# Top-k attention and SwiGLU on one core: the fourth FFN block's gate and value computed in halves of 128 tokens

## The chip, the core and the metric

One core of one Trainium2 chip runs the whole program. The metric is device microseconds for one execution of the kernel, from a median of a few runs. The engines that matter are PE (TensorE, the matrix engine, whose weight loads are listed apart as PEld), DVE (VectorE), ACT (ScalarE), POOL (GpSimd) and SP (SyncE, which here issues nearly all DMAs). Each engine executes its own list of instructions in the order in which the program wrote them, and waits where an instruction needs the result of another engine.

## The reference

Everything is fp32. For 8 batches of 8 heads, 576 positions and head size 64, each row of scores keeps its 32 largest entries and is softmaxed over these. The result, laid out as 4608 tokens of 512 features, goes through a gated feed-forward network of width 1536.

```python
def _attn_ref(q, k, v):                       # (8, 8, 576, 64) each
    scores = scale * np.matmul(q, k.transpose(0, 1, 3, 2))
    kth = np.partition(scores, -top_k, axis=-1)[..., -top_k:-top_k + 1]   # top_k = 32
    scores = np.where(scores >= kth, scores, -1000000000.0)
    scores = scores - np.max(scores, axis=-1, keepdims=True)
    attn = np.exp(scores)
    attn = attn / (np.sum(attn, axis=-1, keepdims=True) + 1e-09)
    return np.matmul(attn, v)

def _moe_ref(x, w_gate, w_val, w_out):        # x: (4608, 512), d_ff = 1536
    g = x @ w_gate
    silu = g * (1.0 / (1.0 + np.exp(-g)))
    val = x @ w_val
    return silu * val @ w_out
```

## The kernel before

**Attention in units.** The attention is cut into 160 units (`units`, line 281): 8 batches, 5 query tiles each (four of 128 rows, and a last one of 64), and 4 pairs of heads. A full unit handles two heads of 128 query rows; a unit of the last query tile packs two heads of 64 rows and is called a half unit here (one 576-wide row set in place of two). The loop at line 870 walks over the units. In turn `n` DVE selects the top 32 of unit `n` (`select`, lines 347 and 351: four rounds of MAX8 with three rounds of MATCH_REPLACE8 between them), ACT turns the scores of unit `n-1` into exponentials (`weigh`, lines 374 and 379), DVE and POOL or ACT normalize them (`normalize`, lines 392 to 399), and PE transposes the weights of unit `n-2` (`turn`, line 412). Every second turn, the even ones, PE also computes the scores of the next two units (`scores`, lines 325 and 308) and the products with V of the units `n-4` and `n-3` (`values`, line 448). ACT copies these last into the token buffer `xT` (line 465).

**FFN in blocks and pieces.** The 4608 tokens form 18 blocks of 256 (`BLK`). A block has six steps of gate and value: for each 256 of the 1536 columns, 8 matmuls for the gate and 8 for the value (line 604, weight tile 128x128, moving operand 128x256), which ACT takes out of PSUM with tanh, half and plus one (lines 637 to 639) or with a copy (line 644), and POOL multiplies into `h` (lines 640 and 645). Then the output product is made as seven quarter products (line 670, "quarters"), with sums and differences of `h` made by POOL (lines 677 to 718). A matmul of fp32 operands stands in the profile as two records. The work is written as generators which give a "piece" at each `yield`: four 128x256 matmuls of gate or value, or three of a quarter.

**Blocks in halves.** Blocks below `HALVED` compute gate and value in two passes of 128 tokens by `feed_half(kb, t)`: each pass has three groups of four 128-column slices for the gate and three for the value (line 517, moving operand 128x128), and the evictions at lines 537 to 539 and 544 cover 128x512 elements just as those of a whole block do. A piece is then eight 128x128 matmuls. Blocks 0 and 1 are fed through `early_jobs`; from block 2 on `feed(kb)` runs, and at line 592 it takes the two half passes first if `kb` is below `HALVED`. The output quarters are the same for both kinds; `pair` (line 621) only picks the tile.

**What sets the order.** Nothing is scheduled by the hardware: at fixed places in each turn `pieces` runs as many pieces as a credit allows (`share`, line 813, fills it by an estimate of what the turn's other PE work leaves free). A block may begin only when enough of its tokens have been written by `values`; line 793 asks this:

```python
if not todo or done.get(todo[0], 0) < tokens(todo[0], int(todo[0] >= HALVED)):
    return 0
```

A whole block waits for all its 256 tokens (second argument 1), a halved block for its first 128 (second argument 0), and its second pass waits for the rest itself at line 504. Credit that finds no piece is lost, as the credit of the next turn is capped at that turn's share plus one. In the last turns the credit is 8, and what is left of the FFN runs after the last unit.

Block 3, the fourth, covers the tokens 192 to 447 of batch 1. Its first half needs query tile 2 of that batch, its second half needs query tile 3. Block 5 is followed by block 6, whose tokens are the next at which `feed` has to wait.

Of the kernel before, what the change touches and what calls it, by code (L numbers as in the profile page):

```python
# [25 lines left out]
def kernel(  # L26
# [46 lines left out]
    MS = MC // 2  # L73
    MQ = MC // 2
    NBLK = B * S // BLK
    HALVED = 3
    AHEAD = 8 * NHP
    scale = 1.0 / float(D) ** 0.5
    assert D == 64 and R == 64 and H * D == DM and DM == 512 and B * S % BLK == 0
# [410 lines left out]

    halves_of = {(kb, t): [] for kb in range(HALVED) for t in range(2)}
    fed, told = [], []

    def tokens(kb, t):

        ends = [0]
        for b in range(B):
            ends += [b * S + min(S, (qt + 1) * P) for qt in range(J + 1)]
        end = min(x for x in ends if x >= kb * BLK + (t + 1) * P)
        return NHP * min(end - kb * BLK, BLK)  # L500
# [86 lines left out]
    def feed(kb):  # L587
# [3 lines left out]

        if kb in range(2, HALVED):
            for t in range(2):
# [27 lines left out]
        def pair(m, t):  # L621

            if kb < HALVED:
                return halves_of[kb, t][m // 4][:, m % 4 : m % 4 + 2, :]
# [4 lines left out]

        for s in range(MS if kb >= HALVED else 0):  # L630
            h = ffn.tile([P, 2, BLK], FP32, tag="h", name="h", bufs=MS + 1)
# [145 lines left out]
    def piece():  # L777
# [13 lines left out]
        while True:  # L791
            if not current:
                if not todo or done.get(todo[0], 0) < tokens(todo[0], int(todo[0] >= HALVED)):
                    return 0
# [189 lines left out]
```

## Time and profile before

| | |
|---|---|
| median of 3 runs | 1713.33 us (1712.2 to 1714.15) |
| the profiled execution's own time | 1712.03 us |
| its span, first to last instruction | 1710.2 us |
| granted TensorE clock, mean | 0.978 |
| PE busy | 1647.4 us (96%) |
| DVE busy | 1476.5 us (86%) |
| ACT busy | 1259.5 us (74%) |
| POOL busy | 799.0 us (47%) |

Times in the profile are microseconds from the first instruction. "Busy" is the union of an engine's records; matmuls overlap each other in the records (a new one starts before the last has drained), so the spacing of PE work is better read from the chain of waits, which gives for each step a start, a length and what ran. Groups by line give a count, busy time, mean duration of one record, and the idle time of the engine just before these instructions. Windows give the busy time of each engine in a stretch of time.

### The profile page before, as it was taken

What the parts mean: (1) busy time and instruction counts of PE and PEld (TensorE: products, weight loads), DVE (VectorE), ACT (ScalarE), POOL (GpSimd) and SP (SyncE); (2) the same over time, 40 slices, a digit from 0 to 9 for tenths busy, and PEclk for the clock granted to TensorE, in tenths of its full rate; (3) what the DMA queues carried; (4) which work ended last, traced back from release to release, by engine and by line L of the source; (5) the groups of instructions that cost most, each with busy time, mean ns of one, the idle gap of its engine ahead of it and who ended that gap; (6) DMA issues with size and microseconds to landing.
All of it is one profiled execution on the core that took longest, in us unless ns stands there. A gap on an engine that the chain in (4) does not pass through costs nothing.

```text
span 1710.2 us, 32128 instructions
## 1 busy us (share of the span) xinstructions
PE 1647.4 (96%) x11600; PEld 1398.2 (82%) x11600; DVE 1476.5 (86%) x3311; ACT 1259.5 (74%) x2901; POOL 799.0 (47%) x914
## 2 busy tenths in 40 slices
PE   5588999999999999999999999999999999999999
PEld 3477698987888887888888888888888888888887
DVE  7999899998989899997999989998999979999400
ACT  7899887877767787768676887777777778676531
POOL 4798545352444425353535334444344433535434
PEclk6699999999999999999999999999999999999999
DMA  7533120003000030001200030000400011000000
GB/s 210 139 112 99 29 72 2 14 1 79 22 13 1 15 86 14 1 8 42 51 14 1 13 74 27 2 13 2 98 1 13 2 44 29 13 2 13 1 13 13
DMA packets 109310, 59.74 MB, mean 35 GB/s; under 512 B 88544, under 2 KB 96992, under 8 KB 109152
## 3 DMA queue, kind: packets, MB, share of 16 engines
q1 hardware_dynamic: 108016, 57.37, 12.9%
q8 instruction: 91, 1.49, 0.4%
q14 instruction: 67, 0.55, 0.1%
q10 hardware_dynamic: 1136, 0.33, 0.1%
HBM read 48.23 MB, written 9.44 MB: 34 GB/s over the span
## 4 chain that ended last, share of the span: by engine, by line
PE 88%; DVE 5%; ACT 4%; DMA 1%; POOL 1%; issue 1%; SPq 0%; POOLq 0%; ACTq 0%
PE f L604 37%; PE x_ps L670 10%; PE av L448 9%; PE s L325 8%; PE y_ps L670 8%; PE etps L412 7%; PE f L517 6%; DVE m L347 2%; DVE e L351 2%; PE kqps L271 1%; PE o_ps L569 1%; PE s L308 1%; ACT e L379 1%; DVE size L124 1%; ACT e L374 0%
## 5 line engine op out<-in xcount | busy, mean ns | idle before, releaser
L347 DVE MAX8 m<-e 128x8 f32<-128x576 f32 x864 | 617.9, 755 | 3.3
L351 DVE MATCH_REPLACE8 e<-m,e 128x576 f32<-128x576 f32 x576 | 425.4, 748 | 0.0
L604 PE MATMUL f<-xT,wg 128*128 128x256 f32 x1440 | 335.9, 382 | 1.3 <-ACT xT L465 1.3
L604 PE MATMUL f<-xT,wv 128*128 128x256 f32 x1440 | 331.4, 380 | 0.0
L604 PEld LDWEIGHTS f<-xT,wg 128*128 128x128 f32 x1440 | 268.9, 190 | 49.0 <-issue 13.1
L604 PEld LDWEIGHTS f<-xT,wv 128*128 128x128 f32 x1440 | 268.2, 190 | 37.5 <-issue 3.8
L640 POOL TENSOR_TENSOR h<-h,half_g 128x512 f32<-128x512 f32 x90 | 114.7, 1275 | 349.2 <-ACT h L639 349.2
L330 ACT ACTIVATE sc<-s 128x288 f32<-128x288 f32 x512 | 170.4, 431 | 105.2 <-PE s L325 104.6
L413 ACT COPY et<-etps 128x512 f32<-128x512 f32 (+1 forms) x448 | 183.6, 486 | 66.0 <-PE etps L412 65.6
L379 ACT ACTIVATE e<-e,bias 128x576 f32<-128x576 f32 x288 | 221.7, 780 | 12.7 <-POOL bias L362 9.7
L374 ACT ACTIVATE e<-sc,m 128x576 f32<-128x576 f32 x288 | 212.3, 792 | 0.6 <-DVE m L347 0.5
L351 DVE MATCH_REPLACE8 e<-m,sc 128x576 f32<-128x576 f32 x288 | 212.6, 748 | 0.0
L412 PE MATMUL etps<-ident,e 128*128 128x128 f32 x1312 | 178.2, 280 | 33.7 <-POOL e L399 15.0
L347 DVE MAX8 m<-sc 128x8 f32<-128x576 f32 x288 | 204.0, 747 | 7.5 <-ACT sc L330 7.5
L412 PEld LDWEIGHTS etps<-ident,e 128*128 128x128 f32 x1312 | 156.2, 144 | 54.7 <-POOL e L399 19.2
L645 POOL TENSOR_TENSOR h<-h,val 128x512 f32<-128x512 f32 x90 | 114.8, 1275 | 155.0 <-ACT val L644 152.4
L325 PE MATMUL s<-kqT 64*128 64x288 f32 x1024 | 169.2, 441 | 13.7 <-ACT sc L330 7.5
L399 POOL TENSOR_TENSOR e<-e,tot 128x576 f32<-128x576 f32 x140 | 161.1, 1154 | 28.5 <-DVE tot L393 28.2
L448 PE MATMUL av<-et,v 128*64 128x128 f32 (+1 forms) x2560 | 158.0, 268 | 0.0
L448 PEld LDWEIGHTS av<-et,v 128*64 128x64 f32 x2560 | 137.7, 140 | 5.9 <-ACT kqT L268 2.7
L325 PEld LDWEIGHTS s<-kqT 64*128 64x128 f32 x1024 | 94.2, 190 | 58.3 <-issue 18.4
L397 ACT ACTIVATE e<-e,tot 128x576 f32<-128x576 f32 x148 | 119.1, 805 | 21.7 <-DVE tot L393 21.6
(86 smaller groups left out, 2249.1 us busy)
## 6 DMA issues: line engine op xcount, KB each, us to landing
v<-in_v_dram SPq DMA_DIRECT2D x32, 256.0 KB, 3.3
kq_in<-in_k_dram SPq DMA_DIRECT2D x63, 128.0 KB, 2.8
kq_in<-in_q_dram SPq DMA_DIRECT2D x63, 128.0 KB, 2.9
w<-in_moe_w_gate_dram SPq DMA_DIRECT2D x12, 512.0 KB, 3.8
w<-in_moe_w_val_dram SPq DMA_DIRECT2D x12, 512.0 KB, 3.8
w<-in_moe_w_out_dram SPq DMA_DIRECT2D x12, 512.0 KB, 3.5
out_dram<-o SPq DMA_DIRECT2D x38, 128.0 KB, 2.4
out_dram<-o SPq DMA_DIRECT2D x16, 256.0 KB, 2.5
```

The lines of the kernel that those rows point to most:

```text
L325: nc.tensor.matmul(ps[:, 0:half], slab[d, q0 : q0 + P], slab[d, k0 : k0 + half])
L330: nc.scalar.mul(sc[:, i * half : (i + 1) * half], ps[:, 0:half], scale)
L347: nc.vector.max(m[:, t, 8 * r : 8 * r + 8], cur[:, hs])
L351: nc.vector.match_replace(e[:, hs], m[:, t, 8 * r : 8 * r + 8], cur[:, from_[t]], LOWEST)
L374: nc.scalar.activation(e[:, hs], sc[:, at], AF.Prelu, bias=m[:, t, TOP_K - 1 : TOP_K], scale=-1.0, alpha=SMALL,)
L379: nc.scalar.activation(e[:, hs], e[:, hs], AF.Exp, bias=bias[:, t : t + 1], scale=-1.0 / SMALL, accum_out=tot[:, t : t + 1],)
L399: nc.gpsimd.tensor_tensor(e[:, hs], e[:, hs], tot[:, t : t + 1].to_broadcast([P, S]), ALU.mult)
L412: nc.tensor.transpose(ps[:, c * P : (c + 1) * P], e[:, k0 : k0 + P], ident[:])
L413: nc.scalar.copy(et[:, c0 : c0 + cn, :], ps[:, 0 : cn * P].rearrange("p (c j) -> p c j", c=cn),)
L448: nc.tensor.matmul(av[d, i, 0:ql], weights_, moving, start=c == (0 if last else J), stop=c == (J if last else J - 1),)
L604: nc.tensor.matmul(ps[:, i, :], w[:, kc, m * P : (m + 1) * P], x[:, kc, :], start=(kc == 0), stop=(kc == KC - 1),)
L670: nc.tensor.matmul(ps, lhsT, T[i][m], start=m == 0, stop=m == MQ - 1)
```

## The change

`HALVED` goes from 3 to 4. Block 3 leaves the path with line 604 and takes `feed_half(3, 0)` and `feed_half(3, 1)`: 192 matmuls with a moving operand of 128x128 in place of 96 with 128x256. The same constant stands in the test at line 793, so block 3 may begin when its first 128 tokens are there, and the tiles that the quarters read are those of the two half passes (line 623).

```diff
@@ -73,7 +73,7 @@
     MS = MC // 2
     MQ = MC // 2
     NBLK = B * S // BLK
-    HALVED = 3
+    HALVED = 4
     AHEAD = 8 * NHP
     scale = 1.0 / float(D) ** 0.5
```

## The prediction

> **What bounds the kernel now.** I read the page first: which engine is busy, when, and what the last chain lies on.
>
> ```profile
> span 1710.2 us, 32128 instructions
> PE 1647.4 (96%) x11600; PEld 1398.2 (82%) x11600; DVE 1476.5 (86%) x3311; ACT 1259.5 (74%) x2901; POOL 799.0 (47%) x914
> ...
> PE 88%; DVE 5%; ACT 4%; DMA 1%; POOL 1%; issue 1%; SPq 0%; POOLq 0%; ACTq 0%
> ```
>
> PE carries 88% of the chain. So time is PE work plus the few places where PE waits. What one FFN matmul costs comes from the chain of waits at two stretches without a break, one in a halved block and one in a whole one (start, length, what):
>
> ```profile
> 252.48 5.36 PE f L517 x48
> ...
> 258.82 7.15 PE f L517 x64
> ...
> 428.47 6.91 PE f L604 x32
> ```
>
> A 128x128 record takes 7.15/64 = 111.7 ns, a 128x256 record 6.91/32 = 215.9 ns, so two halves are 3.5% dearer than one whole. Next, where PE does wait near block 3: the chain from 388 us on, and the windows (busy time by engine; the second window is the same two half units one batch later, the third a stretch that I need below).
>
> ```profile
> 388.95 0.58 ACT o L759
> 389.54 0.72 ACT e L374 x2
> ...
> 390.78 1.61 ACT e L379 x4
> 392.39 0.31 ACT xT L465 x2
> 392.71 1.21 ACT sc L315 x4
> ...
> 395.77 1.20 PE etps L412 x9
> ```
> ```profile
> 388.80:398.10 9.30, 7.15 (x84) 5.60 (x83) 7.55 (x17) 9.05 (x23) 3.14 (x4) 1.00 0.29 67
> 585.80:599.30 13.50, 13.50 (x118) 11.62 (x117) 7.86 (x20) 10.43 (x25) 4.32 (x6) 1.00 0.03 6
> 662.30:704.00 41.70, 39.38 (x270) 32.88 (x269) 41.56 (x98) 32.87 (x79) 13.36 (x15) 1.00 0.04 14
> ```
>
> At 388.8 block 2 has ended and block 3 has not all its tokens: no FFN matmul runs, PE is busy 7.15 of 9.30 us, and the path crosses ACT. In the window of the next batch FFN work fills the same half units and PE has no gap. In the third, DVE is busy 41.56 of 41.70 us. The chain there:
>
> ```profile
> 657.23 0.74 PE s L325 x4
> 657.96 1.30 ACT sc L330 x4
> ...
> 662.12 0.17 DVE tot L392
> ...
> 674.57 0.82 ACT e L374 x2
> ...
> 675.92 1.61 ACT e L379 x4
> 677.53 0.16 ACT xT L465
> 677.73 2.86 PE f L604 x12
> ```
>
> This is the other place where FFN work runs out: block 5 has ended and block 6 waits for tokens. From 662.12 to 677.73 the path is DVE's selection and then ACT's exponentials; PE stands aside until `xT` is written at 677.7.
>
> **The change part by part.**
>
> *Dearer matmuls.* Line 517 has 576 gate and 576 value records in three blocks, line 604 has 1440 and 1440 in fifteen: 384 records a block against 192. Block 3's gate and value go from 192 x 215.9 ns = 41.5 us to 384 x 111.7 ns = 42.9 us: +1.4 us of PE work. It lies on PE where PE is the path, so it counts in full.
>
> [...]
>
> The rows of this trace decide: in the unbroken stretch at 258.82 the records of line 517 follow each other every 111.7 ns although PEld shows a mean of 196 ns for each of their loads, so the loads are hidden by overlap here.
>
> *Evictions and sums.* ACT's four operations and POOL's two products for 128x512 elements keep their number and size: line 537 to 539 and 544 take 596, 597, 639 and 586 ns, line 637 to 639 and 644 take 597, 595, 635 and 584 ns. The POOL sums of the quarters take 727 to 731 ns in halved and whole blocks alike. Nothing, by these rows; no cover is needed.
>
> *Block 3 begins earlier.* Building both kernels gives each engine's order of instructions. I count FFN matmuls between one `values` group on PE and the next, halves counted as half a whole one, with the time of before at which each stretch begins:
>
> | stretch begins | 370.0 | 388.8 | 398.1 | 415.0 to 658.3 | 658.3 | 671.8 |
> |---|---|---|---|---|---|---|
> | before | 30 | 0 | 20 | 382 | 12 | 36 |
> | after | 34 | 16 | 16 | 378 | 0 | 36 |
>
> Before 658.3 the changed kernel has done 12 matmuls more; these are taken from the stretch at 658.3, because block 6 still waits for the same tokens. From 671.8 to the end the order on PE is the same. So the change moves 24 records, 24 x 215.9 ns = 5.2 us, from the stall at 658 into the stall at 389, and PE's work up to 658.3 grows by 5.2 + 1.4 = 6.6 us.
>
> *The stall at 389 is filled.* PE is idle 9.30 - 7.15 = 2.15 us there. Ends of records overlap, so this is a lower reading. The stretch at 585.8 has the same attention work on PE and 16 matmuls (32 records, 6.9 us) besides, and takes 13.5 us; without them it would take 6.6, and the stretch at 388.8 takes 9.3: 2.7 us idle. I take 2.4. Bounds: nothing is filled (ACT is busy 9.05 of 9.30 us and gets a gate and a value eviction, 596+597+639+586 ns = 2.4 us, in front of the `et` copies on which `turn` waits), or all 2.7. I take the value near the upper end, because the row nearest to it, the window at 585.8 with FFN work in the same half units, shows PE 13.50 of 13.50 us with ACT at 10.43.
>
> *The stall at 658 grows.* The changed kernel takes 5.2 us of PE work out of a stretch whose path is DVE and ACT. DVE needs about 9.95 us for a full unit and runs them end to end there; PE's first FFN matmul waits for `xT`, which ACT writes after the exponentials, which follow DVE's MAX8. With less to do PE waits longer for the same signal. Bounds of what is won back: nothing, or all 5.2 us. I take nothing, as the third window leaves DVE 0.14 us of idle in 41.7.
>
> *What starts that chain.* It starts with PE's scores at 657.23, at the end of a stretch that is on PE, so DVE begins late by what PE is late.
>
> *New small gaps.* By the order, two stretches on the way lose work (457.8: from 34 matmuls to 27, after one of 39; 585.8: from 16 to 12). There PE runs ahead of DVE for a moment. The stretch of before with the same 12 matmuls in half units, 781.9 to 794.4, was busy 12.05 of 12.50 us. 0 to 1.0 us; I take 0, since PE can run well ahead before it waits: at 669.18 it made scores for the unit after the one that DVE began at 675.11.
>
> *DMA queue.* On SP the four stores of block 2 (2.43 us of issuing at 390.99) now come before two loads into `vlast` (389.31), which land in about 2.1 us and are first used by `av` at 457.8. Cover: over 60 us. If it were gone, at most those 2.4 us. POOL and ACT get their work in another order, with no queue of DMAs behind it (ACT issues none here).
>
> *Sum.* +6.6 - 2.4 + 0 + 0 = +4.2 us, all of it present by 658 and unchanged to the end, as nothing behind differs. Against the profiled execution 1712.03 + 4.2 = 1716.2; that execution lies 1.3 us under the median shown, so against the median 1713.33 + 4.2 = 1717.5 us, +0.25%. A measurement of this kernel tells about 0.2%, 3.4 us, from no change, so this lies just beyond.
>
> **The rivals.**
>
> A, *the lead is kept* (ends not slower). Having less to do at 658, PE would start block 6 earlier, and all or part of 5.2 us comes back. For it: PE at 677.73 does wait, and the first four matmuls of block 6 could be done before. Against it: DVE and ACT between 662 and 677. All won back: 6.6 - 2.4 - 5.2 = -1.0, 1712.3 us. From 0.8 us won back the result is within 0.2%. Chance 0.2.
>
> B, *ACT keeps the stall at 389*. The 2.4 us of eviction stand before the copies that PE needs, the idle stays: +6.6, and up to 1.0 of small gaps: 1719.9 to 1720.9. For it: ACT at 9.05 of 9.30. Against it: the window at 585.8. Chance 0.12.
>
> C, *halves are far dearer, or do not take place as I read the order*. With another 20% on 42.9 us it would be 1717.5 + 8.6 = 1726.1; without any effect 1713.3. For it no row. Chance 0.04.
>
> **How the numbers follow.** My own case has 0.64, with its own range from +3.2 (2.7 filled, 0.7 won back) to +5.2 (new gaps): 1716.5 to 1718.5. The range given adds B's end at 1720 and the half of A that wins back up to 3.3 us, so it starts at 1714.2. Faster by over 0.2% needs a gain of 3.4 us, which no case holds: 0.03. Within 0.2%: all of A but a little, and the lower edge of my own case, where 0.8 us decide: 0.27. Slower: 0.70.
>
> **What would show it.** In the changed profile: line 517 with 768 gate records; FFN matmuls in the half units at 389 and PE without the 2.15 us of idle there; the scores that start the DVE chain at about 661.4 in place of 657.2, and the first matmul of block 6 behind `xT` at about 682 in place of 677.73, with some 5 us more PE idle before it; then every later step late by the same amount. I am wrong if that wait shrinks instead (A), if PE still waits for ACT near 390 (B), or if records of line 517 no longer follow at 112 ns (C).

## The result, and the profile after

| | before | after |
|---|---|---|
| median of 6 runs | 1713.18 us (1712.2 to 1714.15) | 1720.42 us (1718.59 to 1721.38) |
| ratio to before, 95% interval | 1 | 1.0039 [1.003, 1.0049] |
| the profiled execution's own time | 1712.03 us | 1721.09 us |
| its span | 1710.2 us | 1719.3 us |
| granted TensorE clock, mean | 0.978 | 0.977 |

The changed kernel is slower by 7.2 us in the medians and by 9.06 us between the two profiled executions. The forecast was 1717.5 us: the sign is right, the size is 2.9 us short, and the median lies 0.4 us above 1720 us, where the range ends; as a ratio to before it is 1.0039, as 1720 is to the 1713.33 us from which the forecast started.

The head of the page and the groups of PE's instructions, after:

```profile
span 1719.3 us, 32509 instructions
PE 1652.4 (96%) x11792; PEld 1407.0 (82%) x11792; DVE 1476.8 (86%) x3311; ACT 1259.7 (73%) x2901; POOL 798.5 (46%) x914
```
```profile
L604 PE MATMUL f<-xT,wg 128*128 128x256 f32 x1344 | 316.7, 385 | 0.8 <-ACT xT L465 0.8
...
L517 PE MATMUL f<-xT,wg 128*128 128x128 f32 x768 | 92.3, 277 | 3.7 <-ACT xT L465 3.7
```

Line 517 has its 768 gate records, and PE has 192 records more, worth 1.4 us by the prediction's row. The rest of the 9.06 us is time in which PE stands aside, or records that take longer. To find where, both traces are cut at the same events, the beginning of each `values` group on PE (line 448), and the stretches compared one by one. "Work" is the difference in PE's instructions by the order, each at the record spacing of the prediction (111.7 and 215.9 ns).

| stretch of before begins | before, us | after, us | difference | of it work |
|---|---|---|---|---|
| 0 to 370.0 | | | +1.4 | 0 |
| 370.0 | 18.88 | 20.66 | +1.79 | +1.79 |
| 388.8 | 9.28 | 13.75 | +4.48 | +7.15 |
| 398.1 | 16.88 | 15.38 | -1.49 | -1.49 |
| 415.0 | 21.47 | 22.01 | +0.53 | +0.54 |
| 436.5 | 21.37 | 23.96 | +2.60 | +1.66 |
| 457.8 | 21.52 | 19.61 | -1.91 | -3.02 |
| 501.7 to 585.8 | | | +2.14 | +1.73 |
| 585.8 | 13.52 | 12.47 | -1.05 | -1.73 |
| 599.3 to 658.3 | | | -0.36 | 0 |
| 658.3 and 671.8 | 37.42 | 39.76 | +2.35 | -5.18 |
| 695.8 to 1643.7 | | | +0.1 | 0 |
| 1643.7 to the end | 66.53 | 65.04 | -1.49 | 0 |

Three of the rows hold no instruction that differs: the first (+1.4, all of it before 176 us), the small one after 695.8, and the last (-1.49). The first and the last are differences between executions. A kernel of the experiments that is before but for an edit at turn 160, near the end, is itself 1.1 us later than before at 176 us. The last is one of the clock (0.50 from 1643.74 to 1647.15 us in before, 1.00 at the same place after), to which the experiments come back. What the change does stands between 370 and 695.8: +6.7 us up to the stall at 658, and +2.35 us in it.

*The stall at 389.* The window after, the same two half units:

```profile
392.00:405.80 13.80, 13.80 (x150) 12.80 (x148) 8.13 (x20) 10.51 (x26) 4.36 (x6) 1.00 0.20 45
```

The columns are the stretch and its length, then the busy time and count of PE, PEld, DVE, ACT and POOL, the granted clock, the DMA share and GB/s. PE was busy 7.15 of 9.30 us; now it is 13.80 of 13.80. 7.15 us of work took 4.48 us more: the stall is filled, and it held 2.7 us.

*The end of block 3.* Windows and PE's waits after, in the two stretches in which block 3 passes from gate and value to the quarters:

```profile
443.20:467.10 23.90, 23.45 (x202) 20.80 (x200) 22.08 (x51) 15.40 (x38) 13.03 (x16) 1.00 0.10 26
467.10:486.80 19.70, 18.86 (x132) 15.57 (x130) 17.42 (x42) 14.18 (x35) 9.81 (x15) 1.00 0.00 1
```
```profile
PE x_ps L670 <- POOL h L718: 0.8, 1, 0.8
PE x_ps L670 <- POOL h L685: 0.5, 1, 0.5
```

In before PE has no gap in the same stretches (21.30 of 21.30 and 21.50 of 21.50 us). Here it waits 1.3 us for POOL's sums, as the trace counts it, and the two stretches together are 2.1 us longer than their work (0.94 and 1.11). The chain after shows what is late at the first of the two waits:

```profile
450.49 3.59 PE f L517 x32
454.11 0.60 ACT h L537
...
458.55 0.48 ACT val L544
...
459.16 1.28 POOL h L545
460.44 2.06 POOL xT L677 x3
...
463.76 0.69 POOL h L685
...
464.49 1.56 PE x_ps L670 x6
```

The last gate of block 3 is ready at 454.1, its value is taken out at 458.6, after a unit's exponentials, then come POOL's product and sums, and PE's quarter product at 464.5 waits for them. The second wait has another chain:

```profile
477.12 1.62 ACT e L379 x4
478.74 0.49 ACT p L704
...
480.84 1.23 POOL p L657
482.06 0.69 POOL h L718
...
482.80 2.86 PE x_ps L670 x12
```

Here ACT takes out an earlier quarter product (`p`) after the exponentials of the next unit, and POOL adds that product up (L657) before it makes the sum (L718) that PE waits for.

*A smaller wait.* In the stretch that begins at 585.8 in before and at 595.3 here, PE waits for a copy by ACT:

```profile
607.50 0.33 PE L264 MATMUL kqps<-ident,kq_last 128*128 128x128 f32 x1 [0.46 <-ACT et L413]
```

*The stall at 658.* The chain after:

```profile
665.35 0.74 PE s L325 x4
666.09 1.30 ACT sc L330 x4
...
670.24 0.17 DVE tot L392
...
682.70 0.82 ACT e L374 x2
...
684.05 1.61 ACT e L379 x4
685.66 0.16 ACT xT L465
...
685.86 5.20 PE f L604 x12
```

DVE's chain begins at 670.24 in place of 662.12, +8.12, and PE's matmuls behind `xT` at 685.86 in place of 677.73, +8.13. The 15.6 us between them stay as they were; nothing of the removed 5.2 us of PE work comes back. New is the length of the last line: twelve records that took 2.86 us take 5.20. The windows and PE's timeline after tell why:

```profile
674.00:676.00 2.00, 2.00 (x11) 1.67 (x11) 2.00 (x6) 2.00 (x5) 0.00 (x0) 0.50 0.00 0
680.00:682.00 2.00, 0.39 (x5) 0.23 (x2) 1.97 (x9) 1.35 (x4) 1.15 (x1) 1.00 0.00 0
684.00:690.00 6.00, 5.17 (x13) 3.64 (x12) 6.00 (x13) 3.18 (x11) 0.00 (x0) 0.50 0.00 0
```
```profile
673.61 2.18 PE L412 MATMUL etps<-ident,e 128*128 128x128 f32 x9 [1.75 <-ACT e L397]
...
681.77 1.65 PE L325 MATMUL s<-kqT 64*128 64x288 f32 x8 [1.61 <-ACT sc L330]
...
685.86 5.20 PE L604 MATMUL f<-xT,wg 128*128 128x256 f32 x12 [0.83 <-ACT xT L465]
```

With less to do PE has gaps of 1.75, 1.61 and 0.83 us here, and the granted clock goes to 0.50, the second time just where PE is the path again. That is the +2.35 us, and the prediction did not speak of it. The clock in such places differs from one execution of a kernel to the next (from 684 to 690 us 0.50 here, 1.00 in a repeat), which the comparisons below have to keep apart; the last section comes back to it.

### The profile page after: what moved, and what is told of

It is laid out like the page before. It is cut to its first block, busy times and chain, and to the rows that moved or that the text cites. A ratio compares the mean times of both kernels' runs of the same rounds, so it can differ in the third digit from the quotient of the medians.

```text
span 1719.3 us, 32509 instructions
## 1 busy us (share of the span) xinstructions
PE 1652.4 (96%) x11792; PEld 1407.0 (82%) x11792; DVE 1476.8 (86%) x3311; ACT 1259.7 (73%) x2901; POOL 798.5 (46%) x914
## 4 chain that ended last, share of the span: by engine, by line
PE 87%; ACT 5%; DVE 4%; POOL 1%; DMA 1%; issue 1%; SPq 1%; POOLq 0%; ACTq 0%
PE f L604 34%; PE x_ps L670 10%; PE av L448 9%; PE s L325 8%; PE f L517 8%; PE y_ps L670 7%; PE etps L412 7%; DVE e L351 2%; DVE m L347 2%; PE kqps L271 1%; ACT e L379 1%; PE o_ps L569 1%; PE s L308 1%; ACT et L413 1%; ACT e L374 1%
## 5 line engine op out<-in xcount | busy, mean ns | idle before, releaser
L604 PE MATMUL f<-xT,wg 128*128 128x256 f32 x1344 | 316.7, 385 | 0.8 <-ACT xT L465 0.8
L604 PE MATMUL f<-xT,wv 128*128 128x256 f32 x1344 | 308.1, 380 | 0.0
L604 PEld LDWEIGHTS f<-xT,wg 128*128 128x128 f32 x1344 | 252.4, 192 | 47.0 <-issue 13.5
L604 PEld LDWEIGHTS f<-xT,wv 128*128 128x128 f32 x1344 | 250.9, 190 | 33.3 <-issue 1.9
L640 POOL TENSOR_TENSOR h<-h,half_g 128x512 f32<-128x512 f32 x84 | 107.0, 1274 | 341.4 <-ACT h L639 341.4
L413 ACT COPY et<-etps 128x512 f32<-128x512 f32 (+1 forms) x448 | 183.9, 487 | 63.1 <-PE etps L412 63.0
L412 PE MATMUL etps<-ident,e 128*128 128x128 f32 x1312 | 178.8, 281 | 35.0 <-POOL e L399 15.6
L645 POOL TENSOR_TENSOR h<-h,val 128x512 f32<-128x512 f32 x84 | 107.1, 1275 | 140.1 <-ACT val L644 137.6
```

Source lines behind the costliest of these rows:

```text
L412: nc.tensor.transpose(ps[:, c * P : (c + 1) * P], e[:, k0 : k0 + P], ident[:])
L413: nc.scalar.copy(et[:, c0 : c0 + cn, :], ps[:, 0 : cn * P].rearrange("p (c j) -> p c j", c=cn),)
L604: nc.tensor.matmul(ps[:, i, :], w[:, kc, m * P : (m + 1) * P], x[:, kc, :], start=(kc == 0), stop=(kc == KC - 1),)
```

## The experiments

My theory after the result: of 6.7 us that do not depend on the clock, the dearer halves are 1.4 and the work moved out of the stall at 658 is 5.2; 2.7 are given back by the stall at 389, and 2.1 are new waits for POOL at the end of block 3, with 0.7 at 585.8. The rivals: the halves themselves cost the 2.1 too; the half clock is what makes the result larger than forecast; PE still mattered between 662 and 677.

In some of these kernels PE gets extra matmuls, `busy(k)`: k products of 128x256 into a PSUM tile that nothing reads. They add work and change no result.

**Halves, but the old start.** Block 3 keeps its halves and begins, as before, when all its tokens are there.

```diff
-                if not todo or done.get(todo[0], 0) < tokens(todo[0], int(todo[0] >= HALVED)):
+                if not todo or done.get(todo[0], 0) < tokens(todo[0], int(todo[0] >= 3)):
```

> Block 3 stays in halves but waits for all its 256 tokens as before, so only the price of the halves is left. If the loss beyond the predicted sum comes from work that was moved into the stall at 389 us and is missed later, this kernel costs only the 384 records of 111.7 ns against 192 of 215.9 ns: +1.4 us, ratio 1.0008, and its stretches before 389 and from 658 on look like those of the kernel before, with a granted clock of 1.00 at 680 us. Rival: halves themselves make the block's end late (the last value tile, POOL's sums, PE's quarters); then the same two waits of about 1 us each appear when block 3 passes to its quarters: +3.4 us, ratio 1.0020.

Measured: 1712.94 us (11 runs), ratio 0.9999 [0.999, 1.0007]. By stretches against before it is +0.29, +0.53, +0.53 and +0.06 from 398 to 480, +1.4 in all, and in each the difference is the work to 0.01 us. PE waits for POOL nowhere at the end of the block. So the halves cost what the record spacing says, and the waits for POOL do not come from them. In the medians 1.4 us can't be told from nothing. The stall at 389 is back:

```profile
390.10:399.20 9.10, 6.96 (x83) 5.42 (x81) 7.34 (x17) 9.01 (x23) 2.91 (x4) 1.00 0.29 68
```

**The stall at 658 filled with extra matmuls.** The changed kernel, with twelve extra matmuls, 5.2 us, in the turn that lost them.

```diff
         pieces(2)
+        if n == 64:
+            busy(6)
...
         pieces(1)
+        if n == 64:
+            busy(6)
```

> The changed kernel with 12 matmuls of 128x256 that nobody reads put into turn 64, in the stall before block 6. In the changed kernel's profile the clock falls to 0.50 at 684 to 690 us and the first 12 records of block 6 take 5.20 us, not 2.6. If the missing work cost that clock, the clock stays at 1.00 with these matmuls, the 12 records take 2.6 us, and the kernel is 2.3 us faster than the changed one (about +4.9 us over before, ratio 1.0028) although it does 5.2 us more PE work. If the slow records have another cause: no change, ratio 1.0040. If PE's work were on the path there, against the reading that DVE and ACT are: 5.2 us slower than the changed kernel, ratio 1.0070.

Measured: 1719.5 us (5 runs), ratio 1.0034 [1.0022, 1.0047]. The two stretches take 12.95 + 24.47 = 37.42 us, as in before, against 39.76. The window and the chain of this kernel:

```profile
684.00:690.00 6.00, 4.63 (x26) 4.03 (x26) 5.98 (x15) 4.42 (x14) 0.00 (x0) 1.00 0.00 0
```
```profile
685.33 0.16 ACT xT L465
...
685.53 2.86 PE f L604 x12
```

5.2 us of PE work put back into the stall cost nothing, so its path is DVE and ACT, and taking them out could win nothing: this is the prediction's step, shown from the other side. The clock stays at 1.00 in this trace, and the 2.35 us are gone from it. That the extra matmuls did this is not shown by one trace, since a repeat of the changed kernel kept its clock there without them, as the next run shows. The median is 0.9 us lower, but the two intervals overlap.

**The changed kernel again**, without an edit.

> The changed kernel once more, on the chip of these runs, to compare with: ratio 1.003 to 1.005 of the kernel before, the clock at 0.50 after the stall before block 6 in its profile.

Measured: 1720.23 us (5 runs), ratio 1.0042 [1.003, 1.0055]. This profiled execution kept its clock in the stall:

```profile
684.00:690.00 6.00, 4.63 (x26) 3.84 (x25) 6.00 (x14) 4.43 (x14) 0.00 (x0) 1.00 0.00 0
```

The gaps of PE are there as in the first trace, the two stretches take 37.41 us, as in before with 5.2 us more of PE work, and the expectation of 0.50 missed. In return its last stretch took 66.57 us, as before's (66.53), where the first trace has 65.04. The half clock is thus not a fixed part of the change: with the same gaps it came in the stall in the first trace and not in this one (0.50 and 1.00 from 684 to 690 us), and before the last block in this one and not in the first (0.75 and 1.00 from 1649 to 1655 us).

**Both places filled, in the changed kernel and in before.** This takes the clock out of the comparison: the changed kernel with the extra matmuls of above and five more before the last block, and before with these five alone.

```diff
             run(turn(n - TURN))
+        if n == 160:
+            busy(5)
```

> The changed kernel with both gaps filled by matmuls that nobody reads: 12 in turn 64 (the stall before block 6) and 5 in the gap before the last block. What is left of its distance to the kernel before with the same fill of the last gap is then free of the clock. Theory: +6.7 us over that one (4.2 of moved and dearer work, 2.1 of waits for POOL where block 3 ends, 0.4 of smaller gaps), about 1718.0 us. Rival (the clock after the stall is most of what my sum missed): about +4.5 us.

> The kernel before with 5 matmuls of 128x256 in the gap before the last block, where PE waits for ACT. Theory: the last stretch takes 65.0 us in all executions and the kernel is 1 to 2 us faster, ratio 0.999, with less spread. Rival (the 2.4 us between the two paced kernels had another cause): no change.

Measured: 1718.91 us (6 runs), ratio 1.0033 [1.0021, 1.0045], and 1711.92 us (11 runs), ratio 0.9992 [0.9983, 1.0001]. The last stretch takes 65.06 and 65.05 us. The two medians differ by 7.0 us; in its stretches from 370 to 658 the changed one repeats the list above to within 0.02 us, 6.7 us in the sum, and the stall at 658 adds -0.49 + 0.49 = 0. The theory's 6.7 stands, and the rival that the clock is most of the miss falls: with it out of the way the distance is 7.0 in place of 7.2. With the five matmuls before the last block the clock of before is 1.00 from 1641 to 1645 us in its trace, and its last stretch takes 65.05 us where it took 66.53. The times fit that: all eleven runs of before with them took at most 1712.54 us, and ten of the sixteen of before on the same chip took longer.

**The end of block 3 shifted.** The changed kernel with 0.6 less credit per turn in turns 40 and 41, so that the gate and value end a few matmuls later.

```diff
         beside = 5.8 if n < AHEAD else 6.25
+        if 40 <= n < 42:
+            beside -= 0.6
```

> The changed kernel with 0.6 less credit in turns 40 and 41, so that block 3 passes to its quarters about 6 matmuls later within the turns; the stretch at 658 stays without FFN work. In the changed kernel PE waited there twice for POOL (0.5 us for L685 at 464, 0.8 us for L718 at 483; the two stretches took 2.1 us more than their work). If the waits come from where the block's end falls among the turns, most of these 2.1 us go and the kernel is 1 to 2 us faster than the changed one. Rival (they belong to a block in halves at any place, against the reading of the run with the late start): same time as the changed kernel.

Measured: 1716.33 us (11 runs), ratio 1.0018 [1.0009, 1.0026], 3.9 us under the changed kernel on the same chip. Against the first trace of the changed kernel the stretches that begin at 415.0, 436.5 and 457.8 change by -1.79, -1.75 and +1.48 = -2.06 us, with equal work in the sum, and PE waits for POOL no more. So the 2.1 us hang on the place in the turns at which the block ends. The other 1.8 us of the 3.9 stay open: the stall takes 12.36 + 25.05 = 37.41 us here and in the repeat. (Here the clock was at 0.50 from 672.9 to 679.7 us, where PE is not the path, so it cost nothing.) Against the changed kernel with both places filled, 1718.91 us on another chip, the distance is 2.6 us, so most of the rest would fit a clock that is lost less often in this kernel; that was not tried.

**Block 6 in halves in place of block 3.** The changed kernel would lose nothing at 658 if block 6 could begin with its first half. Here blocks 0, 1, 2 and 6 are halved and block 3 is whole.

```diff
-    HALVED = 4
+    HALVED = (0, 1, 2, 6)
...
-        if kb in range(2, HALVED):
+        if kb >= 2 and kb in HALVED:
...
-                if not todo or done.get(todo[0], 0) < tokens(todo[0], int(todo[0] >= HALVED)):
+                if not todo or done.get(todo[0], 0) < tokens(todo[0], int(todo[0] not in HALVED)):
```

> Blocks 0, 1, 2 and 6 in halves, block 3 whole: the start is moved out of the stall at 658 us, not into the one at 389. By the order of instructions 24 matmuls move into the stretch at 658 and 18 of them are missing from the stretch at 739, where block 7 now waits for tokens; that stretch keeps 15 matmuls, more than the 12 that stood in the stall at 658 before. Theory (a lead is worth what the units after the next stall are stretched by PE): the 3.1 us of idle at 658 are filled, 1.4 us of dearer halves are added, and of the 7.8 us missing at 739 nearly all come back, since PE there stretches units 74 to 77 by over 6 us in the kernel before: about -1 us, ratio 0.9995, between 0.999 and 1.001. Rival (whatever is taken ahead of a token wait is lost at it, as at 658 in the changed kernel): 7.8 + 1.4 - 3.1 = +6 us, ratio 1.0035.

Measured: 1713.7 us (11 runs), ratio 1.0003 [0.9994, 1.0012]. PE is full through the stall:

```profile
666.00:682.00 16.00, 16.00 (x133) 15.09 (x130) 15.97 (x37) 10.33 (x22) 5.91 (x7) 1.00 0.09 34
```

From 658 to 739.5 us of before this kernel falls 5.9 us behind before, and then the stretch in which block 6 would still have had work goes from 21.23 to 13.44 us: -7.8, all of it work that had been done earlier. In the next stretch 1.6 us of it come back, as PE waits 1.4 us for `xT`. So the same move, from a later wait to an earlier one, can be nearly free. There the units after it were stretched by PE, and missing work shortens them. At 658 the units already go at DVE's pace, and missing work leaves a gap.

**Less FFN before the two stalls.** If work is late at one place because there is none, credit held back before it should fill the stall without any halves. Before, with 0.5 less credit per turn in the six turns ahead of each stall; in the first kernel the second stretch is turns 58 to 63, in the other turns 52 to 57.

```diff
         beside = 5.8 if n < AHEAD else 6.25
+        if 30 <= n < 36:
+            beside -= 0.5
+        if 58 <= n < 64:
+            beside -= 0.5
```
```diff
+        if 52 <= n < 58:
+            beside -= 0.5
```

> The kernel before with HALVED 3; the credit of turns 30 to 35 and 58 to 63 is 0.5 lower, so 9 matmuls move from the stretch at 347 to the one at 389 and 9 from the stretches at 614 and 636 to the one at 658. No work is added. Theory: both stalls have PE idle (2.7 and 3.1 us) that 3.9 us of work each can fill, and the stretches that lose the work are on PE: -2 us at the first (DVE's own pace of 9.7 to 9.95 us a unit takes back some), -2.5 us at the second, -4.5 us in all, ratio 0.9974. Rival: the stretches that lose the work are held by DVE, so nothing comes back: 0, ratio 1.000; if the added work delays ACT's copies in the half units, +1 to +2 us.

> The kernel before with 0.5 less credit in turns 30 to 35 and 52 to 57: 9 matmuls move into the stall at 389 as in the first paced kernel (there -1.55 us), and 9 move into the stall at 658, now out of stretches at 545 to 636 in which block 5 is still at gate and value. If the first paced kernel lost its second gain because the passage of block 5 to its quarters was squeezed together and PE waited 2.1 us for POOL's L690 and then ran at half clock, the second gain is back: -1.5 - 2.7 = about -4 us, ratio 0.9976. Rival (DVE holds the stretches that lose work): about -1.5 us, ratio 0.9990.

Measured: 1711.85 us (11 runs), ratio 0.9986 [0.9978, 0.9995], and 1709.5 us (8 runs), ratio 0.9978 [0.9967, 0.9988]. In both the first stall gives -3.88 + 2.33 = -1.55 us: nine matmuls moved into it, and 1.55 of its 2.7 us filled. In the first kernel the second shift lost its gain, because a quarter product then waited for POOL's sums, and the clock fell behind that gap; waits and windows of that kernel:

```profile
PE y_ps L670 <- POOL xT L690: 2.1, 1, 2.1
```
```profile
654.00:656.00 2.00, 2.00 (x10) 1.43 (x11) 2.00 (x6) 0.00 (x0) 1.79 (x3) 0.81 0.00 0
656.00:658.00 2.00, 2.00 (x14) 1.10 (x12) 2.00 (x6) 1.11 (x4) 0.00 (x0) 0.50 0.00 0
```

With the second shift six turns earlier, in the other kernel, there is no such wait, the second shift gives another -2.1 us, and the windows of the stall at 658 are full:

```profile
655.30:671.20 15.90, 15.90 (x120) 13.30 (x118) 14.60 (x36) 13.25 (x33) 7.85 (x10) 1.00 0.01 2
671.20:693.60 22.40, 22.40 (x150) 19.02 (x148) 22.33 (x52) 16.56 (x40) 7.80 (x9) 1.00 0.06 25
```

**The same with the gap before the last block filled.** The second of these two kernels with `busy(5)` in turn 160, as above.

> As the second paced kernel, with 5 matmuls of 128x256 that nobody reads in PE's gap of about 2 us just before the last block, where PE waits for ACT's L397. In some profiles the granted clock is 0.5 to 0.7 after that gap and the rest takes 66.5 us, in others it stays at 1.00 and takes 65.0. If a gap of this size is what the clock answers to, the fill keeps the clock in all executions: up to 1.5 us faster than the second paced kernel, with less spread from run to run. Rival: the clock is set by something else: same time, or 0.2 us slower where the fill sticks out of the gap.

Measured: 1707.14 us (5 runs), ratio 0.9968 [0.9955, 0.998], the fastest here. The last stretch goes from 66.55 to 65.04 us, and the extra matmuls lengthen the one before it by 0.17, so the trace gains 1.3 us; the 2.4 us between the medians is no better measure, as the two intervals overlap. The windows at the gap, without the extra matmuls and with them:

```profile
1641.00:1645.00 4.00, 4.00 (x48) 3.54 (x49) 0.00 (x0) 1.02 (x3) 0.00 (x0) 0.60 0.41 94
```
```profile
1641.00:1645.00 4.00, 4.00 (x55) 3.51 (x54) 0.00 (x0) 1.02 (x3) 0.00 (x0) 1.00 0.44 103
```

The clock is what differs: 0.60 and 1.00.

## Why the prediction was right, and where it was too small

- *Dearer matmuls, +1.4*: right, and shown alone by the kernel with halves and the old start.
- *Evictions and sums, 0; DMA queue, 0*: the operations take as long as before, and no wait for the queue appears in the stretches. But the term said that "no cover is needed", and this was wrong: at the end of block 3 PE does wait for these sums, as below.
- *24 records moved, PE work +6.6 up to 658*: right. The work column up to there sums to 6.6.
- *The stall at 389, -2.4*: 2.7, the upper bound of the term. ACT's two evictions did not stand in the way, and rival B, which kept the idle time, is refuted by PE's 13.80 of 13.80 us.
- *The stall at 658 wins back 0*: right. The time from DVE's start to PE's restart stays at 15.6 us, and putting 5.2 us of PE work back cost nothing. Rival A is refuted.
- *New small gaps, 0 with bounds 0 to 1.0*: this is the step that failed. It measured 2.8 us: 2.1 where block 3 passes to its quarters, where PE waits for POOL's sums, and 0.7 at 585.8 (smaller differences cancel). For the second the prediction had the row (12.05 of 12.50 us busy at 781.9) and set it to nothing; PE now waits 0.46 us for ACT's copy (L413) there, as it did in that row. For the first it asked whether PE runs ahead of DVE, and not who waits for whom where a block passes from gate and value to the quarters: the chain gate and value, ACT, POOL's product, POOL's sums, quarter takes about 10 us (454.1 to 464.5 in the chain above), and PE needs other work for that time.
- *Sum*: 6.6 - 2.7 + 2.8 = 6.7 in place of 4.2. The medians with both clock places filled give 7.0; 0.3 of that is within the spread of the runs. That 1720.42 us lies at the end of the range is luck: the range went up to 1720 only for rival B, whose mechanism the trace refutes, and the prediction's own case ended at 1718.5.
- *Unchanged behind 658*: right for the order, and for the time but for the clock. The 2.35 us in the profiled execution were not in the sum at all. In the medians they matter little (7.2 against 7.0): before too loses time to the clock, before its last block (66.53 us for the last stretch, where it is 65.04 with the clock at 1.00), and the changed kernel does not lose it at 658 in every execution.
- *What would show it*: scores at about 661.4 and the first matmul behind `xT` at about 682. They came at 665.35 and 685.86, each 4 us later than written: 2.5 of the sum, and 1.4 of the profiled execution's slower start.

## What to carry to other kernels

Count the bottleneck engine's work between one wait for data and the next: work moved from a later wait into an earlier one pays only for the idle time of the earlier, unless the units after the later one are still stretched by that engine. Where a block's end moves among the other work, look at the longest chain through the other engines at that end, and at what covers it there. A stall can be filled more cheaply than by smaller tiles: less credit in the turns ahead of it leaves work for it (ratio 0.9978), and with five matmuls that nobody reads in the gap before the last stretch of PE work the clock there was 1.00 in place of 0.60 (together 0.9968).

## What the runs showed of the hardware

The granted TensorE clock fell to 0.50 at or soon after gaps of PE of 1.6 to 2.1 us. In the changed kernel it fell at 673.56, as a gap of 1.75 us ended, and at 683.80, 2.0 us after the end of one of 1.61 us (5.20 us for twelve records in place of 2.86); in the first paced kernel at 655.2, after a gap of 2.08 us; in before at 1643.74, after one of 1.78 us (1.5 us of the last stretch). It stayed there for 3.41 and 6.82 us in the changed kernel and for 3.41 us in before:

```profile
673.56:676.97 3.41, 3.36 (x14) 2.35 (x14) 3.41 (x8) 3.41 (x9) 0.09 (x1) 0.50 0.00 0
676.97:683.80 6.83, 5.22 (x56) 4.17 (x55) 6.80 (x17) 3.62 (x9) 1.34 (x2) 1.00 0.01 2
683.80:690.62 6.82, 5.99 (x15) 4.29 (x14) 6.79 (x19) 3.38 (x11) 0.00 (x0) 0.50 0.00 0
690.62:694.00 3.38, 3.38 (x21) 3.02 (x21) 3.38 (x7) 2.90 (x7) 1.22 (x1) 1.00 0.00 0
```
```profile
1640.33:1643.74 3.41, 1.63 (x20) 1.16 (x16) 0.32 (x2) 2.57 (x8) 0.94 (x1) 1.00 0.33 79
1643.74:1647.15 3.41, 3.41 (x44) 3.11 (x44) 0.00 (x0) 0.99 (x3) 0.00 (x0) 0.50 0.33 75
```

The length of the gap alone does not decide it. In before a gap of 1.75 us, which ends at 395.77, left the clock at 1.00 from 388.8 to 398.1 us. Before the last block PE is idle for 1.77 or 1.78 us in eight traces without extra matmuls there: in six of them the clock falls (means of 0.60 to 0.77 over 4 or 6 us at the restart of PE), and in two, the first of the changed kernel and the late start, it stays at 1.00. The same window in the first trace of the changed kernel and in its repeat:

```profile
1649.00:1655.00 6.00, 4.22 (x77) 3.39 (x76) 0.32 (x2) 4.36 (x10) 1.28 (x1) 1.00 0.30 70
```
```profile
1649.00:1655.00 6.00, 4.22 (x52) 3.61 (x51) 0.32 (x2) 3.23 (x9) 0.51 (x1) 0.75 0.39 90
```

What decides between the two was not shown. The fall at 683.8, which cost the 2.35 us, has no cause shown either: PE had resumed at 681.77.

With extra matmuls in the gap the clock was 1.00 in the traces: with five before the last block from 1641 to 1645 us, in before (last stretch 65.05 us) and in the second paced kernel (65.04 us), and with twelve in the stall at 658 from 665.5 to 703 us in the changed kernel, and from 666 to 703.5 us in the one with both places filled, whose last stretch took 65.06 us. In that stall the clock also stayed at 1.00 in one of three executions without them, the repeat of the changed kernel.
